# Attention decode with an MLP beside it: the loop over steps moved from 2.0–62.0 to 0.9–62.9

## The chip, the cores and the metric

The kernel runs on one core of a Trainium2 chip. The core has TensorE (matmuls and transposes), VectorE, ScalarE (activations and copies), GpSimd and SyncE, each with its own instruction stream, and 16 DMA engines that move data between HBM and the on-chip memory. In the profile they are called PE (and PEld for weight loads), DVE, ACT, POOL and SP. The metric is the device time of one execution, in microseconds. Of the kernel before, three runs were taken: 1291.12, 1290.60 and 1290.57, a median of 1290.6.

## The reference

For each of 8 sequences one token is decoded. The token (640 numbers) is normalised, projected to 32 heads of 128, and each head attends over its own cache of 4096 keys and values. The heads' outputs go through `wo`. A small MLP, 640 to 1728 to 640 with a tanh GELU, works on the same normalised token, normalised once more. Both results and the input are added.

```python
xn = _layernorm(x)
q = (xn @ wq) -> (8, 32, 1, 128)
scores = einsum("bhqd,bhkd->bhqk", q, k_cache) * 128 ** -0.5
o = einsum("bhqk,bhkd->bhqd", softmax(scores), v_cache)
y = _layernorm(xn)
mlp = gelu(y @ w1 + b1) @ w2 + b2
out = x + o.reshape(8, 1, 4096) @ wo + mlp
```

All inputs are bf16. K and V are 8 x 32 x 4096 x 128 each, 268 MB apiece. They make up nearly all of the 551.8 MB that the kernel reads.

## The kernel before

The work is cut into 64 steps. Step i takes four heads of one sequence: 4 MB of K and 4 MB of V. On chip each is a tile of 128 partitions; each head has 32 partitions, and every partition holds 128 of the head's 4096 positions. K_sb and V_sb have two buffers each, used in turn. "K3" below is the K load of step 3, "V1" the V load of step 1.

The scores of a step are computed in two ways side by side. VectorE does 88 of the 128 positions of each partition in four chunks of 22 (`dve_chunk`): a multiply with the query spread over the partitions, an addition of the two halves, and a sum. TensorE and ScalarE do the other 40 positions (`jp_of`): TensorE transposes eight positions at a time (`pe_T`), ScalarE evicts them from PSUM (`act_T`), TensorE multiplies with the query (`pe_QK`), ScalarE collects the scores (`act_S`). Then VectorE takes the maximum (`dve_max`, five short instructions), ScalarE takes the exponential and its sums (`act_exp`, four activations), TensorE sums over partitions (`pe_RS`), VectorE takes the reciprocal (`dve_rinv`), TensorE multiplies with V (`pe_PV`, 128 small matmuls), ScalarE evicts that (`act_O`), and GpSimd scales it into oT_sb (`o_norm`). The last step has 64 positions on TensorE, and the last but one has 48.

The order of each engine's instructions is made by the program. Every piece of work is put at a position with `at(pos, fn, ...)` (line 278), one step being 100 long (`Q`); all pieces are sorted by position and recorded, one list of calls per engine. So a position says only what stands in front of what on an engine; the time follows from the waits. Step i's transposes stand at 100i + 5 and after, its chunks at 100i + 10 to 70, its maximum at 100i + 100, its exponential at 100i + 139.5, its PV at 100i + 160, act_O at 184.

SyncE issues nearly all loads, in the order of positions. `load_k(i)`, at 100i - 90, waits until K of step i - 2 has been read by TensorE and by VectorE (its last multiply). `load_v(i)`, at 100i + 20, waits until PV of step i - 2 is done. `load_mlp` at 20 brings the MLP's weights into the tile W_sb, where wq had been, once all queries are made. The output weights come into W_sb at the end, behind V of step 63; they wait for `pe_ox`, since the transposed outputs (O_sb) lie in the same tile.

The MLP has four pieces: `pe_mlp1` (84 matmuls, at 140), `act_gelu` (145), `pe_mlp2` (70 matmuls, 160) and `fin_a` (170), in which VectorE copies the sums, kept with the input in ACC_ps, to resT_sb. That puts them inside step 1.

Behind the attention of the first 28 heads, the outputs are turned: `pe_ot` and `cp_ot` transpose eight heads at a time into rows and evict them (four groups, 28 heads), `pe_ox` transposes them back in another order, and `cp_ox` evicts that. They lie at 6250 to 6292.5 in step 62, among its other work. At the end `fin_b` adds the input and the MLP, `fin_wob` and `fin_woa` multiply with wo, and the result is stored.

Steps 2 to 61 run as a loop with 30 turns of two steps on TensorE, VectorE and ScalarE. `mark` (line 743) notes where position 200 + 200m falls in each engine's calls; `looped` (769) checks that all turns are the same and sets the waits of the first turn to those of the steady pattern; `_replay_loop` emits the body once, with the semaphore counts growing by a register. Steps 0, 1, 62 and 63 are written out. SyncE and GpSimd have no loop.

Of the kernel before, what the change touches and what calls it, by code (L numbers as in the profile page):

```python
# [21 lines left out]
NOW, WHEN = [0], {}  # L22
# [96 lines left out]
def _replay_loop(e, calls, a, b, n):  # L119

    size = (b - a) // n
    assert size * n == b - a and n >= 2
    _replay(e, calls[:a])
    body = calls[a:a + size]
    grow = []
    for j, (name, args, kw, inc, _) in enumerate(body):
        step = 0
        for r in range(1, n):
            name_r, args_r, kw_r, inc_r, _ = calls[a + r * size + j]
            assert name_r == name and inc_r == inc and sorted(kw_r) == sorted(kw), (j, name, name_r)  # L130
            if name == "wait_ge":
                assert args_r[0] is args[0]
                if r == 1:
                    step = args_r[1] - args[1]
                assert args_r[1] == args[1] + r * step and args[1] > 0 and step >= 0, (j, args, args_r)
            else:
                assert [_same(x) for x in args_r] == [_same(x) for x in args], (j, name)
                assert [_same(kw_r[x]) for x in sorted(kw)] == [_same(kw[x]) for x in sorted(kw)], (j, name)
        grow.append(step)
    with e.Fori(0, n) as r:  # L140
        for call, step in zip(body, grow):
            _emit(e, call, call[1][1] + r * step if step else None)
    _replay(e, calls[b:])


def bass_parallel_sum__gqa_block_cached__mixer_channel_mlp__decode_kernel(
# [21 lines left out]
    NQ = NHQ * B  # L168
# [3 lines left out]
    SCALE = float(DH) ** -0.5  # L172
    TPB = 8
    CHMAX = 22
    LOOP0, LOOPN = 2, 30
    NHA = H - HS
    assert NKEY == 128
    NS = 5

    def jp_of(i):  # L180
        return 64 if i == NQ - 1 else 48 if i == NQ - 2 else 40

    def chunks(i):
        jd = NKEY - jp_of(i)
        n = -(-jd // CHMAX)
        return [(jd * c // n, jd * (c + 1) // n) for c in range(n)]

    bank0 = [0]
    for i_ in range(NQ):
        bank0.append(bank0[-1] + jp_of(i_) // TPB)  # L190
# [10 lines left out]
    with ExitStack() as es:  # L201
# [76 lines left out]
        def at(pos, fn, *a):  # L278
            prog.append((pos, len(prog), fn, a))
# [151 lines left out]
        def pe_T(i, t):  # L431
            k = trn[0] % 2
            trn[0] += 1
            s = i % 2
            j0 = NKEY - jp_of(i) + t * TPB
            pe.wait(tk["id"], piece_of("k", i, j0, j0 + TPB))
            TRB[k].use(pe)
            for jj in range(TPB):
                last = pe.transpose(TR_ps[:, k, jj * P:(jj + 1) * P], K_sb[:, s, j0 + jj, :], ident_bf[:, :])
            tk[("T", i, t)] = (k, TRB[k].used(pe, pe.sig(last)))  # L440
            tk[("kt", i)] = tk[("T", i, t)][1]
# [261 lines left out]
        at(13, pe_q, HS, H)  # L703
        at(14, cp_q, HS, H)
        at(20, load_mlp)
        at(140, pe_mlp1)
        at(145, act_gelu)
        at(160, pe_mlp2)
        at(170, fin_a)
        for i in range(NQ):  # L710
            o = i * Q
            last = i == NQ - 1
# [35 lines left out]
            at((LOOP0 + 2 * m) * Q, mark)  # L748
        o = NQ * Q
        for g in range(len(OTG)):  # L750
            at(o - 150 + 10 * g, pe_ot, g)
            at(o - 149.5 + 10 * g, cp_ot, g)
        at(o - 108, pe_ox)
        at(o - 107.5, cp_ox)
        at(o - 60, load_wob)
        for q in range(len(WO_CUT) - 1):
            at(o - 59 + q, load_woa, q)
# [11 lines left out]
        def looped(e, eng):  # L769
            m = list(marks[eng])  # L770
            calls = list(eng.calls)
            size = m[2] - m[1]
            had = {}
            for name, args, _, _, _ in calls[:m[0]]:
                if name == "wait_ge":
                    had[args[0].name] = max(had.get(args[0].name, 0), args[1])
            for j in range(size):
                one, two, three = calls[m[0] + j], calls[m[1] + j], calls[m[2] + j]
                if two[0] == "wait_ge":
                    sem_, value = two[1][0], 2 * two[1][1] - three[1][1]  # L780
                    same = one[0] == "wait_ge" and one[1][0] is sem_
                    need = one[1][1] if same else 0
                    now = one[4]
                    before = had.get(sem_.name, 0)
                    assert value >= min(need, before) and value > 0
                    assert value >= need or need <= before
                    assert value <= max(need, before) or WHEN[sem_.name, value] < now
                    call = ["wait_ge", (sem_, value), {}, None, now]
                    if same:
                        calls[m[0] + j] = call  # L790
                    else:
                        calls.insert(m[0] + j, call)
                        m = m[:1] + [x + 1 for x in m[1:]]
                    had[sem_.name] = max(before, need, value)
            assert {y - x for x, y in zip(m, m[1:])} == {size}, m
            _replay_loop(e, calls, m[0], m[-1], LOOPN)

# [4 lines left out]
        @block.tensor  # L802
        def _(e):
            looped(e, pe)

        @block.vector
        def _(e):
            looped(e, dve)

        @block.scalar  # L810
        def _(e):
            looped(e, act)
# [32 lines left out]
```

## Time and profile before

| what | value |
|---|---|
| median of the runs | 1290.6 us |
| the profiled execution | 1291.13 us, its span 1289.2 us |
| VectorE busy | 1124.3 us (87%) |
| TensorE busy | 677.3 us (53%) |
| ScalarE busy | 588.5 us (46%) |
| read from HBM | 551.8 MB, 428 GB/s over the span |
| K load, issue to landing (median) | 24.7 us |
| V load, issue to landing (median) | 34.1 us |
| mean granted TensorE clock | 0.591 |

All instructions carry line 103, that of the helper which emits the recorded calls, so rows are told apart by their tiles: TR_ps holds transposes of K, S_ps scores (and, at the end, the last product), CH_ps queries, the first MLP product and the sums of the exponentials, ACC_ps the input plus the MLP and later the turned outputs, W_sb the weights. In the rows, "x84" is a number of instructions. "<-" in a row of waits names what ended the wait. SPq is SyncE's queue, on which DMAs are issued. A time "to landing" runs from the issue of a DMA to its arrival, and so includes its wait behind the transfers ahead of it.

### The profile page before, as it was taken

What the parts mean: (1) busy time and instruction counts of PE and PEld (TensorE: products, weight loads), DVE (VectorE), ACT (ScalarE), POOL (GpSimd) and SP (SyncE); (2) the same over time, 40 slices, a digit from 0 to 9 for tenths busy, and PEclk for the clock granted to TensorE, in tenths of its full rate; (3) what the DMA queues carried; (4) which work ended last, traced back from release to release, by engine and by line L of the source; (5) the groups of instructions that cost most, each with busy time, mean ns of one, the idle gap of its engine ahead of it and who ended that gap; (6) DMA issues with size and microseconds to landing.
All of it is one profiled execution on the core that took longest, in us unless ns stands there. A gap on an engine that the chain in (4) does not pass through costs nothing.

```text
span 1289.2 us, 33399 instructions
## 1 busy us (share of the span) xinstructions
PE 677.3 (53%) x14035; PEld 607.1 (47%) x14035; DVE 1124.3 (87%) x1170; ACT 588.5 (46%) x1262; POOL 48.1 (4%) x139
## 2 busy tenths in 40 slices
PE   1765555555545545544544554544544644554558
PEld 1654444444444444544544544544543544543546
DVE  2899988988988988988988988988988988989983
ACT  1453453453553543553543543543544544544553
POOL 0000000000000000000000000000000000000000
PEclk9997555555555565555565655555655555556566
DMA  9999999999999999999999999999999999999998
GB/s 406 426 425 434 428 436 429 433 431 432 431 431 432 431 431 432 435 428 434 430 433 429 434 430 433 430 433 435 428 434 430 434 428 434 431 432 430 432 433 328
DMA packets 20984, 552.09 MB, mean 428 GB/s; under 512 B 2314, under 2 KB 3043, under 8 KB 4068
## 3 DMA queue, kind: packets, MB, share of 16 engines
q1 hardware_dynamic: 20930, 551.80, 99.7%
q8 instruction: 14, 0.23, 0.1%
q14 instruction: 6, 0.05, 0.0%
q10 hardware_dynamic: 34, 0.02, 0.0%
HBM read 551.80 MB, written 0.01 MB: 428 GB/s over the span
## 4 chain that ended last, share of the span: by engine, by line
DMA 60%; DVE 24%; issue 11%; PE 4%; ACT 1%; DVEq 0%; SPq 0%
DMA K_sb<-in_A_k_cache_dram 56%; DVE Y_sb L103 22%; DMA V_sb<-in_A_v_cache_dram 3%; DMA W_sb<-in_B_w_dram 1%; PE S_ps L103 1%; PE CH_ps L103 1%; PE PV_ps L103 1%; DVE Sd_sb L103 1%; PE ACC_ps L103 1%; PE TR_ps L103 0%; DVE ri_sb L103 0%; ACT KT_sb L103 0%; DVEq L101 0%; ACT W_sb L103 0%; ACT P_sb L103 0%
## 5 line engine op out<-in xcount | busy, mean ns | idle before, releaser
L103 ACT ACTIVATE KT_sb<-TR_ps 128x1024 bf16<-128x1024 bf16 x324 | 322.3, 1022 | 428.0 <-PE TR_ps L103 425.7
L103 PE MATMUL TR_ps<-ident_bf,K_sb 128*128 128x128 bf16 x2592 | 304.3, 299 | 372.4 <-DMA K_sb<-in_A_k_cache_dram 371.1
L103 DVE TENSOR_TENSOR Y_sb<-K_sb,qbc_sb 128x2816 bf16<-128x2816 bf16 (+2 forms) x255 | 410.6, 1610 | 92.4 <-DMA K_sb<-in_A_k_cache_dram 92.4
L103 PEld LDWEIGHTS TR_ps<-ident_bf,K_sb 128*128 128x128 bf16 x2592 | 243.5, 137 | 377.7 <-DMA K_sb<-in_A_k_cache_dram 376.3
L103 DVE TENSOR_REDUCE Sd_sb<-Y_sb 128x22 f32<-128x1408 bf16 (+2 forms) x255 | 412.4, 1617 | 8.7
L103 DVE TENSOR_TENSOR Y_sb<-Y_sb 128x1408 bf16<-128x1408 bf16 (+2 forms) x255 | 233.3, 915 | 8.7
L103 PE MATMUL PV_ps<-P_sb,V_sb 128*128 128x4 bf16 x8192 | 228.0, 166 | 7.1 <-DMA V_sb<-in_A_v_cache_dram 4.8
L103 PEld LDWEIGHTS PV_ps<-P_sb,V_sb 128*128 128x128 bf16 x8192 | 225.8, 104 | 9.1 <-DMA V_sb<-in_A_v_cache_dram 6.8
L103 PE MATMUL S_ps<-qrep_sb,KT_sb 128*128 128x4 bf16 x2592 | 123.2, 171 | 75.3 <-ACT KT_sb L103 71.2
L103 PEld LDWEIGHTS S_ps<-qrep_sb,KT_sb 128*128 128x128 bf16 x2592 | 101.4, 105 | 125.2 <-ACT KT_sb L103 121.9
L103 ACT ACTIVATE P_sb<-Sd_sb,NB_sb 32x128 bf16<-32x128 f32 x256 | 147.2, 575 | 6.0 <-DVE NB_sb L103 1.3
L103 ACT ACTIVATE oU_sb<-PV_ps 128x4 f32<-128x4 f32 x63 | 10.9, 173 | 205.8 <-PE PV_ps L103 205.8
L103 PE MATMUL CH_ps<-rs_sb,ones_f 128*128 128x4 f32 x128 | 37.1, 360 | 128.4 <-ACT P_sb L103 124.5
L103 PEld LDWEIGHTS CH_ps<-rs_sb,ones_f 128*128 128x128 f32 x128 | 31.8, 309 | 134.3 <-issue 80.6
L103 POOL TENSOR_TENSOR oT_sb<-oU_sb,ri_sb 128x4 bf16<-128x4 f32 x63 | 31.5, 500 | 1185.5 <-ACT oU_sb L103 1170.3
L103 ACT ACTIVATION_READ_ACCUMULATOR P_sb<-Sd_sb,NB_sb 32x1 f32 x256 | 63.7, 249 | 0.0
L103 ACT ACTIVATE Sd_sb<-S_ps 32x40 f32<-32x40 f32 (+2 forms) x256 | 49.1, 192 | 3.1 <-PE S_ps L103 0.8
L103 ACT ACT_TABLE_LOAD x33 | 42.3, 1283 | 7.5 <-issue 5.8
L103 ACT ACTIVATE qbc_sb<-TR_ps 128x128 bf16<-128x128 f32 x64 | 17.8, 278 | 24.4 <-PE TR_ps L103 22.7
L103 DVE TENSOR_REDUCE mx_sb<-Sd_sb 128x1 f32<-128x128 f32 x64 | 18.3, 286 | 4.4 <-ACT Sd_sb L103 2.0
L103 POOL COPY qrep_sb<-qT_sb 128x128 bf16<-128x128 bf16 x64 | 19.2, 301 | 36.9 <-PE S_ps L103 22.2
L103 PE MATMUL CH_ps<-xT_sb,W_sb 128*128 128x8 bf16 (+1 forms) x230 | 11.1, 179 | 16.4 <-DMA W_sb<-in_A_wq_dram 11.0
(63 smaller groups left out, 152.4 us busy)
## 6 DMA issues: line engine op xcount, KB each, us to landing
K_sb<-in_A_k_cache_dram SPq DMA_DIRECT2D x64, 4096.0 KB, 24.7
V_sb<-in_A_v_cache_dram SPq DMA_DIRECT2D x63, 4096.0 KB, 34.1
W_sb<-in_A_wq_dram SPq DMA_DIRECT2D x1, 5120.0 KB, 15.5
V_sb<-in_A_v_cache_dram SPq DMA_DIRECT2D x2, 2048.0 KB, 23.6
W_sb<-in_B_w_dram SPq DMA_DIRECT2D x1, 2160.0 KB, 16.9
W_sb<-in_B_w_dram SPq DMA_DIRECT2D x1, 2080.0 KB, 21.8
W_sb<-in_A_wo_dram SPq DMA_DIRECT2D x2, 640.0 KB, 22.9
W_sb<-in_A_wo_dram SPq DMA_DIRECT2D x1, 960.0 KB, 22.5
```

The source lines that it names most:

```text
L103: inst = getattr(e, name)(*a, **k)
```

## The change

The loop's marks move from 200 + 200m to 90 + 200m, and it has 31 turns instead of 30: it begins nine tenths into step 0 and ends nine tenths into step 62. What stands before position 90 and behind 6290 stays written out.

For that, what happens only once has to leave the loop's stretch. The four MLP pieces go from 140–170 to 80–88, in front of the loop. Step 62 gets 40 positions on TensorE and 88 on VectorE as all others. The turning of the outputs goes from 6250–6292.5 to 6290.5–6299.5, behind the loop and in front of step 63. `looped` now rebuilds the first turn from the pattern of the second: waits that only the first turn has are put ahead of the loop (`early`), and the others take the steady pattern's counts.

```diff
-    LOOP0, LOOPN = 2, 30
+    LOOP0, LOOPN = 0.9, 31
...
     def jp_of(i):
-        return 64 if i == NQ - 1 else 48 if i == NQ - 2 else 40
+        return 64 if i == NQ - 1 else 40
...
         at(20, load_mlp)
-        at(140, pe_mlp1)
-        at(145, act_gelu)
-        at(160, pe_mlp2)
-        at(170, fin_a)
+        at(80, pe_mlp1)
+        at(82, act_gelu)
+        at(84, pe_mlp2)
+        at(88, fin_a)
...
         for g in range(len(OTG)):
-            at(o - 150 + 10 * g, pe_ot, g)
-            at(o - 149.5 + 10 * g, cp_ot, g)
-        at(o - 108, pe_ox)
-        at(o - 107.5, cp_ox)
+            at(o - 109.5 + 2 * g, pe_ot, g)
+            at(o - 109 + 2 * g, cp_ot, g)
+        at(o - 101, pe_ox)
+        at(o - 100.5, cp_ox)
...
+            first, body, nxt = calls[m[0]:m[1]], calls[m[1]:m[2]], calls[m[2]:m[3]]
+            start, made, early, k = first[0][4], [], [], 0
+            for j, (two, three) in enumerate(zip(body, nxt)):
+                if two[0] != "wait_ge":
+                    while first[k][0] == "wait_ge":
+                        k += 1
+                    made.append(first[k])
+                    k += 1
+                    continue
...
+                    for name, call in group.items():
+                        if name not in steady and had.get(name, 0) < call[1][1]:
+                            assert WHEN[name, call[1][1]] < start
+                            early.append(call)
+                            had[name] = call[1][1]
+                sem_, value = two[1][0], 2 * two[1][1] - three[1][1]
...
+                made.append(["wait_ge", (sem_, value), {}, None, now])
+                had[sem_.name] = max(before, need, value)
+            calls[m[0]:m[1]] = early + made
```

(`o` is 6400, the end of the 64 steps. The old body of `looped`, which kept the first turn's calls in place and changed or inserted waits among them, is replaced by the new one.)

More of the change, by code (lines that the diff above doesn't have):

```diff
@@ L776, in looped @@
                     had[args[0].name] = max(had.get(args[0].name, 0), args[1])
[L777 to L794, printed above, removed]
+            first, body, nxt = calls[m[0]:m[1]], calls[m[1]:m[2]], calls[m[2]:m[3]]
@@ new lines, in looped @@
+            start, made, early, k = first[0][4], [], [], 0
[6 more added lines that the diff above has]
+                    continue
+                if j == 0 or body[j - 1][0] != "wait_ge":
+                    group, at_ = {}, k
+                    while first[at_][0] == "wait_ge":
+                        group[first[at_][1][0].name] = first[at_]
+                        at_ += 1
+                    now = first[at_][4]
+                    steady, jj = set(), j
+                    while body[jj][0] == "wait_ge":
+                        steady.add(body[jj][1][0].name)
+                        jj += 1
+                    for name, call in group.items():
[4 more added lines that the diff above has]
+                sem_, value = two[1][0], 2 * two[1][1] - three[1][1]
+                need = group[sem_.name][1][1] if sem_.name in group else 0
+                before = had.get(sem_.name, 0)
+                assert value > 0, (j, sem_.name, value, need)
+                assert value >= need or need <= before
+                assert value <= max(need, before) or WHEN[sem_.name, value] < now, (j, sem_.name, value, need)
+                made.append(["wait_ge", (sem_, value), {}, None, now])
+                had[sem_.name] = max(before, need, value)
@@ L795, in looped @@
+            calls[m[0]:m[1]] = early + made
+            grew = len(early) + len(made) - len(first)
+            m = [m[0] + len(early)] + [x + grew for x in m[1:]]
             assert {y - x for x, y in zip(m, m[1:])} == {size}, m
```

## The prediction

> **What bounds the kernel now.** First the page's top lines, to see whether an engine or the transfers fill the time.
>
> ```profile
> span 1289.2 us, 33399 instructions
> DVE  2899988988988988988988988988988988989983
> DMA  9999999999999999999999999999999999999998
> GB/s 406 426 425 434 428 436 429 433 431 432 431 431 432 431 431 432 435 428 434 430 433 429 434 430 433 430 433 435 428 434 430 434 428 434 431 432 430 432 433 328
> ```
>
> The transfer row is full in every slice and the rate stands at 428 to 436 GB/s from the fourth slice to the last but one. The two end slices are short: (430-406)/430 and (430-328)/430 of 32.2 us, 1.8 and 7.6 us. So the middle is bound by transfers and nothing done to the loop can shorten it; time can only be lost by letting the queue run dry, or moved in the last few us. Next the waits, the engines' and then the DMA queue's own:
>
> ```profile
> DVE Y_sb L103 <- DMA K_sb<-in_A_k_cache_dram: 92.4, 61, 6.7
> ```
>
> ```profile
> SPq L101 <- DVE Y_sb L103: 1133.6, 62, 20.5
> ```
>
> VectorE waits for K about 92.4/61 = 1.5 us in each step; it follows the transfers. But SyncE waits for VectorE before each K load, since K has two buffers. A late VectorE therefore costs nothing until the queue behind it is empty. How much is queued at the start, the transfer answers of three short windows say (issue to landing, us), with the issues in order of time:
>
> ```profile
> 44.04 0.34 SPq L103 DMA_DIRECT2D K_sb<-in_A_k_cache_dram  x1
> 44.42 0.44 SPq L103 DMA_DIRECT2D V_sb<-in_A_v_cache_dram  x1
> 65.43 0.33 SPq L103 DMA_DIRECT2D K_sb<-in_A_k_cache_dram  x1
> ```
>
> ```profile
> V_sb<-in_A_v_cache_dram SPq DMA_DIRECT2D x1, 4096.0 KB, 31.7
> ```
>
> ```profile
> K_sb<-in_A_k_cache_dram SPq DMA_DIRECT2D x1, 4096.0 KB, 20.4
> ```
>
> V of step 1 (V1), issued at 44.42, lands at 76.1; K3, issued at 65.43, lands at 85.8. The difference, 9.7, is one 4 MB transfer, so nothing was lost between them. Now the chain through the MLP (start, length):
>
> ```profile
> 51.13 7.65 PE CH_ps L103 x84
> 59.33 1.28 ACT L103
> 60.62 0.32 ACT hT_sb L103 x2
> 61.63 1.97 PE ACC_ps L103 x70
> 63.63 0.20 DVE resT_sb L103
> ```
>
> The first MLP product starts at 51.1, when its weights land. VectorE copies the MLP's sums at 63.6, in the midst of step 1's chunks. And the chain at the end:
>
> ```profile
> 1242.64 3.58 PE PV_ps L103 x128
> 1246.22 0.96 PE ACC_ps L103 x8
> 1247.20 1.02 ACT W_sb L103
> 1248.26 1.03 PE ACC_ps L103 x8
> ...
> 1251.66 1.95 PE ACC_ps L103 x28
> 1253.63 0.36 ACT oX_sb L103
> ...
> 1276.28 10.65 PE S_ps L103 x64
> ```
>
> From V61's landing (PV at 1242.64) to the end the chain stays on the engines: transposing, evictions, softmax of the last step, last product. The transfers are done by 1285 (106 GB/s in 1283 to 1285, 0 after it).
>
> **The change, part by part.** *The loop's place.* On TensorE and ScalarE the boundary stays between PV and its eviction, and the next step's transposes, only one step earlier; on VectorE it moves from behind dve_max to in front of it. ScalarE idles 0.2 us at a loop start; VectorE's 1.4 us wait for K hides as much, and if that cover is gone the cost is 0.2 x 31 = 6 us. I take 0. The 31st turn costs nothing more: the same 64 steps run, and the table loads at loop starts go from 30 to 31, while the one for step 0's exp falls away.
>
> *MLP ahead of the loop.* No DMA moves: load_mlp stays at 20. What moves are 154 matmuls, two GELUs and one VectorE copy. On TensorE they now stand in front of step 1's transposes, on VectorE fin_a stands in front of dve_max(0) and all of step 1. In the trace VectorE ends step 0's last reduce at 46.53 and goes on at once. Now it must wait: weights at 51.1; 84 matmuls to 58.8 (7.65); two GELUs 0.32, to 59.2 (the second weights, 21.8 after an issue before 35.9, are there by 57.7); 70 matmuls 2.2, to 61.5; copy 0.2, to 61.75. The table load of 1.28 I count at nothing: ScalarE is free from 42, and the trace shows the exp table loaded at 46.63, ahead of the bias that exp waits for (47.9). If the load stays behind the wait, add 1.3 to 1.8.
> Then dve_max(0), 1.2 (46.62 to 47.82), so step 1's first chunk starts at 62.95 where it was 47.82. From the first chunk's start to the end of the fourth multiply a step without stalls takes 14.1 (69.31 to 83.44). So K1's buffer comes free at 77.1 and K3 is issued at 77.15, 11.7 later than 65.43. Behind VectorE stand SyncE's K3, and V2 behind that. V2's own condition, PV(0), needs step 1's five evictions (about 68), exp (2.4), and 3.6 of matmuls, some 75, and isn't late. TensorE's release of K1 (transposes from 61.5, some 6 us) isn't either.
> The queue holds V1 until 76.1. K3 is issued into a queue that has just run dry, and needs 9.7 plus the latency of such an issue. No row shows it for a K load. From below: x, 10 KB, is issued at 0.74 and read at 2.49, so at most 1.75, taken as the low end. From above: wq, 5 MB, takes 15.5 from issue to landing, and at 432 GB/s 12.1 of that is data, so 3.4. I take the middle, 2.5, as K3 is a big load like wq, but without wq's crowd at the start (262 to 492 GB/s in its first slices). K3 lands at 77.15 + 9.7 + 2.5 = 89.4 and not 85.8: **3.6 us** (2.8 to 4.4) in which nothing is transferred, and which nothing later wins back. The next load is safe: K4 is issued one VectorE step, 17.9, after K3 (62.95 to 80.9 by the same rows), while the queue gains 19.4 of work.
> The Trainium skill, "DMA: Bandwidth & Descriptors", section "Anatomy of one DMA", gives a fixed 2.0 us for a transfer. By it the gap would be 3.1; no run here isolates it.
>
> *Step 62 as the others.* One eviction less on ScalarE (1.02) and four chunks of 22 columns for 20 on VectorE: (1.62+0.89+1.62) - (1.48+0.82+1.49) = 0.34 each, 1.4 in all. VectorE idles 4.1 ahead of K63's first chunk (1252.93), the ScalarE part lies before V61's landing. 0; if the 4.1 were gone, 1.4.
>
> *Outputs turned behind the loop.* Before, the first of four groups was transposed at 1239.9, while V61 was still on its way. Now all four come after PV(61): groups at 1246.2, 1248.3, 1250.4, 1252.5 instead of the last three. A round of eight transposes and one eviction takes 1248.26 - 1246.15 = 2.11. The chain behind it moves as a whole: pe_ox, cp_ox, exp(62) behind cp_ox on ScalarE, the eight evictions of step 63, its softmax, PV(63), the last product. **+2.1.** The output weights, which SyncE issues after pe_ox, are issued at 1255.7 for 1253.6, but V62 and V63 stand ahead of them in the queue, until about 1272, so that is hidden. Leaving the loop is now on the path too: TensorE had 6 us of waiting for K62 to hide it. Nearest row: ScalarE's 0.2 at a loop start; far one: TensorE's 2.3 "issue" stall at 68.76; a gain is excluded, as the group can't start before PV(61) ends. I take **0.2**. On GpSimd only o_norm(61) moves, behind an act_O(61) that now comes ahead of the evictions; nobody waits for it before the last product.
>
> *Clock.* The last 64 matmuls run at half rate until 1279.9, 3.65 after they begin, then at full. Where the step falls next time is open: from the start on, -1.8; one burst (3.4, seen at 1218.5) later, +1.7. I take the row, 0.
> TensorE was 88% busy from 1253 to 1279.9 at a clock of 0.50. The Trainium skill, "TensorE: Matmul & The Clock Gate", Part 1, says a busy window of about 3.4 us, free-running, restores full rate. If thin matmuls don't count as busy, the step comes 3.4 to 6.8 after these wide ones begin, on average 0.7 us dearer than the row. By the rule read plainly, the extra round would run at full rate, as the first group did at 1239.9 (0.61 for 1.0), and cost 1.7 rather than 2.1.
>
> **Sum:** 3.6 + 2.1 + 0.2 = 5.9. The profiled execution took 1291.1 (span 1289.2 and 1.9 around it), 0.5 above the median of 1290.6. So 1297.0 against itself, **1296.5** against the median.
>
> **Rivals.** *Queue never dry:* the MLP's products end earlier, or the latency is overlapped, so that K3 is in time. That needs K3's issue before 76.1 - 2.5 = 73.6, so a chain shorter by 3.6 of its 10.6. For it: TensorE is idle from 40 on and starts fresh. Against: the 84 matmuls ran without a gap. It leaves 2.3: 1292.9, within 0.2% (2.6 us is about what this kernel's measurement can tell) and so not slower. *A longer stall at the start:* the table load behind the wait, and a TensorE "issue" stall (1.3 and 2.3 in the trace) in the unrolled code: 1.8 + 1.3 more, 1299.6. *VectorE's loop branch uncovered:* 6 us more, 1302.5; against it the 1.4 of idle in every step. *A gain:* the end's full clock comes early and the queue stays full: 1292.9 - 1.8 = 1291.1, still no gain; so almost none.
>
> **How the numbers follow.** Forecast 0.70, longer stall 0.15, queue never dry 0.11, branch 0.04. The likeliest one alone goes from 1290.6 + 2.8 + 2.1 - 0.1 = 1295.4 to 1290.6 + 4.4 + 2.1 + 2.3 = 1299.4. Towards the others I widen to 1294.0 and 1300.5. Slower by over 0.2%: 0.70 + 0.15 + 0.04, less a little, 0.88; same 0.10; faster 0.02.
>
> **What would show it.** Right: VectorE idle from 46.5 to 61.5 ahead of the copy of the MLP's sums; K3 issued near 77 and landing near 89; a dip in the rate between 76 and 80 and nowhere else; four rounds of transposes after PV(61). Wrong: no dip (then the rival), or GELU later than 59.5 behind its table load, or TensorE idle on "issue" after PV(61), or idle time of VectorE ahead of its maxima in the loop.

## The result, and the profile after

The changed kernel takes 1296.7 us (median of six runs, 1295.4 to 1297.0), the kernel before 1291.1 in the same comparison: a ratio of 1.0039, with a 95% interval of 1.0029 to 1.0050. The profiled execution took 1296.0, 0.7 below that median; its span is 4.9 longer than the one before. The first lines of its page:

```profile
span 1294.1 us, 33472 instructions
DMA  9989999999999999999999999999999999999997
GB/s 404 427 374 428 432 435 426 436 433 427 435 434 428 431 434 431 430 432 432 431 429 433 432 429 435 432 429 431 435 430 430 435 431 430 432 433 431 428 435 314
```

One slice is new: the third, 64.7 to 97.1, has 374 GB/s where it had 425. (425 - 374)/430 of 32.4 us is 3.8 us of transfers. All later slices but the last are as before within 7 GB/s, and the last is short again. The windows of 2 us around the dip (the last two columns are the transfer engines' busy share and the rate in GB/s):

```profile
72.00:74.00 2.00, 1.58 (x60) 1.52 (x57) 1.93 (x3) 0.00 (x0) 0.00 (x0) 1.00 0.69 291
74.00:76.00 2.00, 0.00 (x0) 0.00 (x0) 2.00 (x3) 0.00 (x0) 0.00 (x0) 1.00 0.12 49
76.00:78.00 2.00, 1.83 (x40) 1.83 (x40) 1.93 (x3) 0.18 (x2) 0.62 (x2) 1.00 0.39 106
78.00:80.00 2.00, 1.74 (x23) 1.47 (x22) 1.90 (x3) 1.94 (x2) 0.04 (x1) 1.00 0.95 328
```

What made it, from three views: VectorE's longest wait in 45 to 120, SyncE's issue of K3, and the transfer answer of 75 to 79, with the time to landing in the last column.

```profile
DVE resT_sb L103 <- PE ACC_ps L103: 14.7, 1, 14.7
```

```profile
76.90 0.33 SPq L103 DMA_DIRECT2D K_sb<-in_A_k_cache_dram  x1
```

```profile
K_sb<-in_A_k_cache_dram SPq DMA_DIRECT2D x1, 4096.0 KB, 12.6
```

VectorE stood 14.7 us for the MLP's sums. K3 was issued at 76.90 instead of 65.43, and landed at 76.90 + 12.6 = 89.5 instead of 85.8.

K3's landing does not hold the whole loss. V2 is next in the queue (issue, then time to landing; first the kernel before, then the changed one):

```profile
69.57 0.33 SPq L103 DMA_DIRECT2D V_sb<-in_A_v_cache_dram  x1
V_sb<-in_A_v_cache_dram SPq DMA_DIRECT2D x1, 4096.0 KB, 26.0
```

```profile
77.27 0.43 SPq L103 DMA_DIRECT2D V_sb<-in_A_v_cache_dram  x1
V_sb<-in_A_v_cache_dram SPq DMA_DIRECT2D x1, 4096.0 KB, 22.8
```

V2 landed at 100.1 instead of 95.6, 4.5 later. From there on every K and V load lands 4.4 to 4.6 later than before, up to K62 (1236.6 for 1232.1). Only the last loads win something back: V61 0.7, and K63 behind it as much again. V61 from issue to landing, before and changed:

```profile
1207.78 34.82 DMA V_sb<-in_A_v_cache_dram
```

```profile
1212.26 34.07 DMA V_sb<-in_A_v_cache_dram
```

It lands 3.7 later. So the gap cost 4.5 as long as the loop runs, and 0.7 of that is gone at its end.

The chain through the MLP shows no table load between the first product and the GELU (1.28 us stood there before):

```profile
51.05 7.66 PE CH_ps L103 x84
58.74 0.05 ACT hT_sb L103
...
59.10 2.13 PE ACC_ps L103 x70
61.26 0.04 DVE resT_sb L103
```

And the chain at the end:

```profile
1246.38 3.57 PE PV_ps L103 x128
1249.95 0.96 PE ACC_ps L103 x8
1250.93 1.02 ACT W_sb L103
1251.99 1.03 PE ACC_ps L103 x8
...
1257.50 1.95 PE ACC_ps L103 x28
1259.47 0.36 ACT oX_sb L103
...
1271.71 3.41 PE PV_ps L103 x128
...
1281.59 10.23 PE S_ps L103 x64
```

PV(61) ends at 1249.95, 3.73 later than 1246.22, as V61 does. The first transpose starts where PV(61) ends, so leaving the loop costs nothing. cp_ox starts at 1259.47 for 1253.63, 5.84 later: 2.11 more. From there 0.95 is won back: PV(62) starts 5.27 later, and the last product takes 10.23 for 10.65. In both stretches this execution had full clock where the one before had half, or earlier (1.00 in the window 1267.4 to 1270.6; before, 0.50 from 1253.0 to 1279.9). 3.73 + 2.11 - 0.95 = 4.89, the difference of the spans.

### The profile page after: what moved, and what is told of

The parts are those of the page before. It is cut to its first block, busy times and chain, and to the rows that moved or that the text cites. A ratio compares the mean times of both kernels' runs of the same rounds, so it can differ in the third digit from the quotient of the medians.

```text
span 1294.1 us, 33472 instructions
## 1 busy us (share of the span) xinstructions
PE 676.5 (52%) x14019; PEld 606.7 (47%) x14019; DVE 1124.9 (87%) x1170; ACT 587.8 (45%) x1261; POOL 51.8 (4%) x139
## 4 chain that ended last, share of the span: by engine, by line
DMA 57%; DVE 26%; issue 12%; PE 4%; ACT 1%; DVEq 0%; SPq 0%; ACTq 0%
DMA K_sb<-in_A_k_cache_dram 53%; DVE Y_sb L103 24%; DMA V_sb<-in_A_v_cache_dram 3%; DMA W_sb<-in_B_w_dram 1%; DVE Sd_sb L103 1%; PE S_ps L103 1%; PE CH_ps L103 1%; PE PV_ps L103 1%; PE ACC_ps L103 1%; ACT KT_sb L103 1%; DVE ri_sb L103 0%; PE TR_ps L103 0%; ACT W_sb L103 0%; DVEq L101 0%; ACT P_sb L103 0%
## 5 line engine op out<-in xcount | busy, mean ns | idle before, releaser
L103 DVE TENSOR_TENSOR Y_sb<-K_sb,qbc_sb 128x2816 bf16<-128x2816 bf16 (+1 forms) x255 | 411.0, 1612 | 83.4 <-DMA K_sb<-in_A_k_cache_dram 83.4
L103 DVE TENSOR_REDUCE Sd_sb<-Y_sb 128x22 f32<-128x1408 bf16 (+1 forms) x255 | 413.0, 1620 | 8.7
L103 DVE TENSOR_TENSOR Y_sb<-Y_sb 128x1408 bf16<-128x1408 bf16 (+1 forms) x255 | 233.5, 916 | 8.7
L103 PE MATMUL S_ps<-qrep_sb,KT_sb 128*128 128x4 bf16 x2584 | 122.6, 171 | 76.3 <-ACT KT_sb L103 72.3
L103 POOL TENSOR_TENSOR oT_sb<-oU_sb,ri_sb 128x4 bf16<-128x4 f32 x63 | 35.6, 566 | 1186.8 <-ACT oU_sb L103 1090.2
L103 ACT ACTIVATE Sd_sb<-S_ps 32x40 f32<-32x40 f32 (+1 forms) x256 | 49.0, 192 | 3.1 <-PE S_ps L103 0.8
L103 PEld LDWEIGHTS CH_ps<-xT_sb,W_sb 128*128 128x128 bf16 (+1 forms) x230 | 9.8, 120 | 22.4 <-DMA W_sb<-in_A_wq_dram 11.3
```

Of the source, the lines that this page charges most:

```text
L103: inst = getattr(e, name)(*a, **k)
```

## The experiments

Each was compared with the kernel before on the same chip. "Above before" is median against median; the positions come from one profiled execution. "K3 late" is its landing against 85.8, "V2 late" and "K62 late" are those landings against 95.6 and 1232.1, and "PV(61) late" is the end of that stage against 1246.22.

| run | K3 issued | K3 late | V2 late | K62 late | PV(61) late | above before | ratio, 95% interval |
|---|---|---|---|---|---|---|---|
| step 62 alone | 65.7 | 0.2 | 0.1 | 0.2 | 0.1 | -0.1 (one time) | – |
| turning alone | 65.3 | -0.1 | -0.2 | 0.2 | 0.4 | 2.1 | 1.0006 to 1.0024 |
| MLP alone | 76.8 | 3.9 | 4.4 | 4.2 | 4.0 | 4.0 | 1.0020 to 1.0041 |
| the whole change | 76.9 | 3.7 | 4.5 | 4.5 | 3.7 | 5.6 | 1.0029 to 1.0050 |
| whole + 2.8 us on VectorE | 79.2 | 6.9 | 6.7 | 6.6 | 5.9 | 8.0 | 1.0046 to 1.0076 |
| whole, copy on ScalarE | 74.4 | 1.7 | 2.0 | 1.8 | 1.1 | 3.1 | 1.0014 to 1.0033 |
| the same, no signal | 74.7 | 2.5 | 2.5 | 2.4 | 1.7 | 3.4 | 1.0014 to 1.0033 |
| the same, GELU wait gone | 73.7 | 1.3 | 1.5 | 1.3 | 0.6 | 2.4 | 1.0014 to 1.0033 |
| whole, three banks | 77.0 | 4.8 | 4.7 | 4.7 | 4.0 | 2.4 | 1.0010 to 1.0029 |
| no signal, three banks, exp first | 74.5 | 2.4 | 2.4 | 2.3 | 1.6 | -0.2 | 0.9992 to 1.0010 |
| the same, GELU wait gone | 74.0 | 1.4 | 1.4 | 1.4 | 0.7 | -0.9 | 0.9987 to 1.0005 |

**The MLP's move alone.**

```diff
-        at(140, pe_mlp1)
-        at(145, act_gelu)
-        at(160, pe_mlp2)
-        at(170, fin_a)
+        at(80, pe_mlp1)
+        at(82, act_gelu)
+        at(84, pe_mlp2)
+        at(88, fin_a)
```

> The kernel before with one part of the change: the four MLP pieces at 80 to 88; the loop stays at 2.0 to 62.0, step 62 and the turning as before. Theory (VectorE waits for the MLP's sums, K3 is issued into an empty queue): K3 issued near 76.9 and landing near 89.5 where it was 85.8, a dip of the rate between 74 and 80, 3.7 us more than before, 1294.8, and the last 40 us of the trace as before. Rival (the loss comes from the loop's new place, above all VectorE's branch in front of the maximum): no dip, 1291.1. Rival (it all comes from the MLP): 1296.7.

Measured: 1295.36 against 1291.35. K3 was issued at 76.80 and took 12.9:

```profile
76.80 0.33 SPq L103 DMA_DIRECT2D K_sb<-in_A_k_cache_dram  x1
```

```profile
K_sb<-in_A_k_cache_dram SPq DMA_DIRECT2D x1, 4096.0 KB, 12.9
```

So the gap is there with the loop at its old place (V2 4.4 late for 4.5). It belongs to the MLP's position, not to the loop's.

**The turning alone.**

```diff
-            at(o - 150 + 10 * g, pe_ot, g)
-            at(o - 149.5 + 10 * g, cp_ot, g)
-        at(o - 108, pe_ox)
-        at(o - 107.5, cp_ox)
+            at(o - 109.5 + 2 * g, pe_ot, g)
+            at(o - 109 + 2 * g, cp_ot, g)
+        at(o - 101, pe_ox)
+        at(o - 100.5, cp_ox)
```

> The kernel before with one part of the change: the outputs are turned at 6290.5 to 6299.5; all else as before. Theory (one more round of eight transposes and an eviction behind PV(61)): all four groups behind PV(61), the last transposes end 5.85 + 3.65 = 9.5 us after PV(61) instead of 7.4, 2.1 us more than before, 1293.2. Rival (the end is hidden behind the output weights' transfers, which end near 1285): 1291.1. Rival (the clock or a stall of TensorE in the written-out code decides at the end): anything from 1290 to 1295, with the 2.1 not to be seen between PV(61) and the first eviction of step 63.

Measured: 1293.42 against 1291.35. Its chain at the end:

```profile
1243.24 3.41 PE PV_ps L103 x128
1246.65 0.96 PE ACC_ps L103 x8
...
1254.20 1.96 PE ACC_ps L103 x28
```

From PV(61)'s end to the end of the last transposes: 1256.16 - 1246.65 = 9.5, as expected; before, 1253.61 - 1246.22 = 7.4. The two parts by themselves make 4.0 + 2.1 = 6.1; the whole change measured 5.6, inside the intervals. That leaves -0.5 for the loop's place and step 62 together, where each of the three differences is uncertain by 1.2 to 1.4 either way.

**Step 62 alone.**

```diff
-        return 64 if i == NQ - 1 else 48 if i == NQ - 2 else 40
+        return 64 if i == NQ - 1 else 40
```

> The kernel before with one part of the change: step 62 with 40 positions on TensorE and 88 on VectorE. Theory: hidden on both engines; VectorE's wait ahead of K63 shrinks from 4.1 to some 2.7, the chain from PV(61) on is the same, 1291.3. Rival (VectorE's later maximum of step 62 delays exp(62)): exp(62) later than 1254.0 and 1292.7.

Measured: 1291.43, one time, against a median of 1291.49. exp(62) starts at 1254.05, cp_ox at 1253.67, where they were 1254.01 and 1253.63. VectorE's wait ahead of K63 is 2.99 for 4.11. In this one execution it is hidden, as said.

**More delay on VectorE.** 14 short sums behind the copy of the MLP's sums:

```diff
             tk["f1"] = ACCB.used(dve, dve.sig(dve.tensor_copy(resT_sb[:, :], ACC_ps[:, 0:DC * B])))
+            dve.wait(tk["consts"])
+            for n in range(14):
+                dve.tensor_reduce(dz_sb[:, n:n + 1], ones_f[:, :], AX.X, ALU.max)
```

> The changed kernel with 14 short sums of 0.29 us (of ones_f, into a scratch tile that nothing reads) on VectorE behind the copy of the MLP's sums, 4.0 us in all. Theory (once K3 is late, each us of VectorE's delay is a us without transfers and nothing wins it back): K3 issued near 80.9, landing near 93.5, 4.0 us more than the changed kernel, 1300.7. Rival (later steps win it back, as VectorE has 1.5 us of idle time in each): 1296.7 to 1298.

Measured: 1299.32. The 14 sums overlap and took 2.8 us, not 4.0, so the dose was smaller than meant. K3 was issued at 79.20, 2.3 later than in the changed kernel, and took 13.5 to land. The windows show the queue wholly dry:

```profile
76.00:78.00 2.00, 1.68 (x38) 1.67 (x38) 2.00 (x3) 0.17 (x1) 0.23 (x1) 1.00 0.00 0
78.00:80.00 2.00, 1.74 (x24) 1.47 (x22) 1.97 (x2) 1.85 (x2) 1.42 (x2) 1.00 0.03 8
80.00:82.00 2.00, 1.95 (x32) 1.69 (x29) 1.93 (x3) 1.53 (x3) 0.00 (x0) 1.00 0.91 262
```

The time rose by 8.0 - 5.6 = 2.4 for those 2.3. K3 lands 3.2 later than in the changed kernel, but V2, K62 and PV(61) only 2.2, 2.1 and 2.2, so a single landing is a rough measure. Later idle time of VectorE won nothing of the delay back.

**The copy on ScalarE**, so that VectorE has no wait for the MLP's sums:

```diff
-            ACCB.use(dve)
-            tk["f1"] = ACCB.used(dve, dve.sig(dve.tensor_copy(resT_sb[:, :], ACC_ps[:, 0:DC * B])))
+            ACCB.use(act)
+            tk["f1"] = ACCB.used(act, act.sig(act.activation(resT_sb[:, :], ACC_ps[:, 0:DC * B], ACT.Copy)))
```

> The changed kernel with one edit: the copy of the MLP's sums (fin_a) is made by ScalarE instead of VectorE, at the same position. Theory (VectorE's wait alone makes the gap): VectorE goes on with step 1 at once, waits later for the sum over partitions of step 0 (TensorE comes to that near 71) and frees K1 near 72.8; K3 is issued at 72.8, just before the queue runs dry at 76.1 less the latency of 2.9; it lands at 85.8 or up to 0.3 later, no dip; 3.7 us less than the changed kernel, 1293.0. Rival (TensorE standing still until the MLP's weights land costs the same by itself, since step 1's transposes come behind it): K3 not before 76, 1296.7.

Measured: 1294.40; K3 at 74.36, not 72.8. VectorE's timeline shows why:

```profile
59.09 0.28 DVE L103 TENSOR_REDUCE mx_sb<-Sd_sb 128x1 f32<-128x128 f32 x1 [12.73 <-ACT hT_sb L103]
```

It did not go on at 46.6. It waited for the GELU. I took that for a semaphore count shifted by the copy's own signal, and took the signal away (whoever needs the copy waits for ScalarE's next signal instead):

```diff
-            tk["f1"] = ACCB.used(act, act.sig(act.activation(resT_sb[:, :], ACC_ps[:, 0:DC * B], ACT.Copy)))
+            act.activation(resT_sb[:, :], ACC_ps[:, 0:DC * B], ACT.Copy)
+            tk["f1"] = ACCB.used(act, (act.sem, act.n + 1))
```

> The changed kernel with the copy of the MLP's sums on ScalarE and without a semaphore signal of its own (whoever needs the copy waits for ScalarE's next signal), so that VectorE's first maximum waits for step 0's scores alone and not for the GELU, as it did in the run with that copy on ScalarE (59.1). Theory (the gap is set by when VectorE frees K1): VectorE goes on at 46.6, stands once at the reciprocal until TensorE's sum near 71, frees K1 near 73.1; K3 issued at 73.1, lands near 86 (0 to 0.5 late), 3.4 us less than the changed kernel: 1293.3. Rival (TensorE's late start on step 1 holds the queue up by itself): K3 at 76 or later and 1296.

Measured: 1294.93, K3 at 74.66: no better, so that explanation fell. The wait is another. GELU is the last reader of the bank that step 0's reciprocal reads; `dve_rinv` therefore waits for it, in the first turn alone, and the changed `looped` puts such waits ahead of the loop (`early`). In the changed kernel it lies hidden under the wait for the sums. TensorE's sum over partitions, for which the reciprocal waits too, comes behind the GELU anyway, so the wait can go:

```diff
         def dve_rinv(i):
-            CHB.use(dve)
+            dve.wait(tk[("rs", i)])
```

> As the run with the copy on ScalarE and no signal, with one more edit: dve_rinv waits for TensorE's sum alone, not also for ScalarE's last use of that PSUM bank (the GELU), a wait that the first turn alone has and that is therefore put ahead of the loop, where it held VectorE until 59.4. Theory (the gap is set by when VectorE frees K1): VectorE goes on at 46.6; its next stand is the reciprocal, which waits for TensorE's sum near 71; K1 free near 73.1; K3 issued at 73.1 instead of 74.7 and landing near 86.5 instead of 88.4, 2 us less than that run: 1293.0, that is the 2.1 us of the turning above the kernel before. Rival (TensorE's late start keeps K3 at 74.7 or later): 1294.9.

Measured: 1293.87. VectorE goes on at 46.41 and its one long stand is the reciprocal:

```profile
46.41 0.29 DVE L103 TENSOR_REDUCE mx_sb<-Sd_sb 128x1 f32<-128x128 f32 x1
...
71.97 0.18 DVE L103 RECIPROCAL ri_sb<-CH_ps 128x4 f32<-128x4 f32 x1 [11.96 <-PE CH_ps L103]
```

K3 is issued at 73.73 and still lands 1.3 late. So VectorE's waits made about two thirds of the gap (V2's lateness 4.5 to 1.5, K3's 3.7 to 1.3). In the medians it is more: 5.6 to 2.4 above before, of which 2.1 is the turning. What is left comes, by the trace, from TensorE's place behind the MLP, through the reciprocal: the rival of these runs has a part of it. No run takes that wait away.

**The turning in three banks**, in the changed kernel:

```diff
+        OTB = [(TRB[0], TR_ps[:, 0, :]), (TRB[1], TR_ps[:, 1, :]), (ACCB, OR_ps), (TRB[0], TR_ps[:, 0, :])]
...
-            ACCB.use(pe)
+            bank, dst = OTB[g]
+            bank.use(pe)
...
-            ACCB.use(act)
+            bank, src = OTB[g]
+            bank.use(act)
```

> The changed kernel with the four groups of transposes put into three PSUM banks by turns (TR_ps 0, TR_ps 1, ACC_ps, TR_ps 0) instead of all into ACC_ps, so that a group need not wait for the eviction of the one before. Theory (the 2.1 us are the serial rounds): from PV(61)'s end to the start of pe_ox 4.8 us (1.0 + 3 x 1.05 + 0.6) instead of 7.6; all behind it 2.8 earlier; 1293.9. The gap at the start stays (K3 at 76.9). Rival (the end is set by the output weights' transfers, over at 1288 in the changed kernel, or by the clock): less than 1 us gained, 1296.

Measured: 1293.93. That is 2.4 above the kernel before, where the changed kernel was 5.6 above it: 3.2 less. The chain from PV(61)'s end to pe_ox:

```profile
1250.17 0.96 PE TR_ps L103 x8
1251.15 3.31 ACT W_sb L103 x4
1254.50 1.95 PE ACC_ps L103 x28
```

4.3 us instead of 7.55, the same 3.2: ScalarE's four evictions run back to back. The cost at the end was the serial rounds. It is also 1.1 less than the 5.4 (1251.66 - 1246.22) of the kernel before.

**Both edits**, and cp_ox behind exp(62): the copy on ScalarE without a signal, the three banks, and

```diff
-        at(o - 100.5, cp_ox)
+        at(o - 99, cp_ox)
```

> The changed kernel with both edits (the copy on ScalarE without a signal; the turning in three banks) and cp_ox behind exp(62) on ScalarE. Theory: no gap at the start, the end 2.8 us shorter than the changed kernel's, and step 63's first eviction at 1254 where it was 1256.4 in the kernel before, since exp(62) no longer stands behind pe_ox. From there the last output weights, which land near 1285.5, limit the end: the last product ends near 1286 where it was 1286.9. 1290.4, 1.0 less than the kernel before; within what can be told apart from it. Rival (the loop's new place costs something of its own that the gap and the end hid): 1292 or more.

Measured: 1291.29 against 1291.49: the same as before, and 0.9 above what I had expected. The expectation took the gap as 0; it was still 2.4 at K3, and V62 landed 1.0 later than before (1263.6 for 1262.6). The chain at its end:

```profile
1271.49 14.36 DMA W_sb<-in_A_wo_dram
1285.90 0.99 PE S_ps L103 x6
```

The last output weights land at 1285.85 and one us later the product is done: there the transfers bound the end. With the GELU wait gone as well:

> As the run with both edits, with the same edit of dve_rinv. In that run the chain at the end is the transfer of the last output weights, which landed at 1285.9, 1 us before the last product ended; so the end follows the gap one for one. Theory: K3 lands 2 us earlier, the last weights 2 us earlier, 1289.3, 0.15% below the kernel before. Rival (the engines' chain becomes the bound again at the end): 1290.5 or more.

Measured: 1290.58 against 1291.44, a ratio of 0.9987 to 1.0005: not told apart from the kernel before. The profiled execution's 1291.6 lies 1.0 above that median. Its chain at the end:

```profile
1253.60 24.36 DMA W_sb<-in_A_wo_dram
1278.01 9.43 PE S_ps L103 x56
```

The weights that landed last no longer bound the end. TensorE stands 0.15 for an earlier piece of them, and then the rest of the last product takes 9.43, at a clock of 0.58 until 1282. So the engines bound the end again, as the rival had it, though not without the transfers.

With both costs mended the kernel can't be told apart from the one before. That alone does not price the loop's place, since the three banks also make the turning 1.1 shorter than it was. Two other readings do: the parts leave -0.5, as said above, and in the changed kernel the loads are 4.5 late at V2 and 4.5 late at K62, so the turns of the loop between them lost nothing. No version tried here beats the kernel before beyond doubt.

## Why the prediction was right

- **K3's delay** was worked out as 77.15 and was 76.90. The weights, the 84 and the 70 matmuls took what the trace before had shown (7.66, 2.13). The table load was hidden as said: in the changed kernel ScalarE makes it at 41.10, ahead of its wait for the product.
- **The latency** of a K load into the dry queue was taken as 2.5, between 1.75 and 3.4. By K3 alone it was 12.6 - 9.7 = 2.9 in the changed kernel, and 2.9 to 4.0 over the runs with a late K3 (12.6 to 13.7 to landing). Over K3 and V2 together it is steadier: from K3's issue to V2's landing these nine runs took 23.0 to 23.5, where two loads in the full queue of the kernel before took 19.45 (V1's landing to V2's). So it was 3.6 to 4.0, above the whole stated range, and this term was some 1.2 too small. The Trainium skill, "DMA: Bandwidth & Descriptors", section "Anatomy of one DMA", gives a fixed 2.0 for a transfer that GpSimd issues; for these loads of SyncE it was more, and the measurement decides.
- **"Nothing later wins back"** held from V2 to K62, 4.5 at both, but not to the end. In the kernel before V61 lands 10.5 after K62, in the changed one 9.8, and so 0.7 came back. The two other runs without a late K3 have 10.4 and 10.3, the nine with a late one 9.8 or 9.9. Why V61 takes longer where K3 is in time is open. The gap was put at 3.6 and is 3.7 at PV(61), but by luck: a latency that was 1.2 short, K3's issue 0.25 early and these 0.7 nearly cancel.
- **The turning** was 2.1 and measured 2.11 in the chain, 2.1 as a run of its own.
- **Leaving the loop**, 0.2, was 0: the first transpose starts where PV(61) ends. VectorE's branch in front of its maximum shows nothing either: in the changed kernel the reduce in front of the second turn ends at 97.32 and the maximum starts at 97.35. Step 62 was 0.
- **The clock** was taken as 0 between -1.8 and +1.7. The profiled execution had 0.95 less at the end, and the median of the runs lies 0.7 above it. Here the full rate came some 2.7 us after the matmuls with 320 columns began (0.51 in the window 1284.2 to 1284.4, 1.00 from there; they start at 1281.59), before it was 3.65. The 3.4 to 6.8 that the prediction estimated from the Trainium skill, "TensorE: Matmul & The Clock Gate", Part 1, was not met by this run; the row was nearer. Nor did the extra round run at full rate, the other reading of that page: eight transposes took 1.03.
- **The sum** was 5.9 and the forecast 1296.5; measured 5.6 between medians, 1296.7, with the kernel before 0.5 slower in this comparison than the 1290.6 that the forecast started from. "Queue never dry" would have needed K3 by 73.6; in the runs with K3 at 73.7 and 74.0 V2 was 1.5 and 1.4 late even so. With a latency of 3.6 to 4.0 the bound is, by estimate, 76.1 less that, some 72.3; the prediction set it too late.
- **What the prediction missed:** that VectorE has two waits ahead of step 1. It named fin_a; the wait for the GELU, moved by `early`, lay under it and came out only when fin_a was taken away.

## What to carry to other kernels

In a kernel bound by transfers, look at each queue's issuing engine: what it waits for, and how much lies in the queue behind that. An engine with idle time in each step may be late by what is queued less the latency of a fresh load (here 3.6 to 4.0), and from there on each us counts in full (here 2.4 for 2.3). Measure a delay on several loads behind the gap, not on the first alone: here the first showed 3.7 and the next ones, up to K62, 4.5. Moving one-off work out of a loop's stretch puts it in front of everything that follows on its engines; the waits count, not the work. And a part that ran under another's transfer costs its whole length where it is put behind the last one that it could hide under.

## What had not been expected of the hardware

A queue that runs dry ends raggedly: in the changed kernel the rate falls to 291 GB/s in 72 to 74 and 49 in 74 to 76, although V1 lands only at 75.9, and it is at 328 in 78 to 80, after K3's issue at 76.90. By an estimate from the 3.6 to 4.0 above, a load must be issued some 4 us ahead of the last landing for nothing to be lost. No run issued K3 between 65.7 and 73.7, so the border itself is not measured. TensorE also stood still for 2.3 to 2.6 us in the middle of PV(0) on nothing that the profile names ("issue"), in the run with the GELU wait gone from about 74.1 to 76.4; it delayed V2's issue there (77.34), but V2 landed 9.9 after K3, near the 9.7 of a full queue.
